# A retention layer and its feed-forward product: the output product in seven block products, and a new order on every engine

## The chip, the cores and the metric

The kernel runs on one core of a Trainium2 chip. The metric is the time of one execution on the device in microseconds (us); lower is better. Five kinds of engine work side by side, each through its own list of instructions in order: PE multiplies matrices (its weight loads are shown apart, as PEld), DVE is the vector engine, ACT the scalar engine, POOL the GpSimd engine, and SP issues the DMA transfers. An instruction starts when it is at the head of its engine's list and the results and buffers that it needs are ready.

## The reference

The inputs are q, k and v of shape (4, 8, 768, 64): batch, heads, tokens, head size. Each head keeps a state that decays by its own factor at each token, and the output of that goes through four weight matrices.

```
gamma = 1.0 - 2.0 ** (-5.0 - np.arange(H, dtype=np.float32))
scale = 1.0 / np.sqrt(D)
for t in range(S):
    state = gamma[None, :, None, None] * state + np.einsum('bhd,bhe->bhde', k[:, :, t], v[:, :, t])
    y[:, :, t] = scale * np.einsum('bhd,bhde->bhe', q[:, :, t], state)
...
x = np.ascontiguousarray(attn_out.transpose(0, 2, 1, 3)).reshape(B * S, H * D)   # 3072 x 512
a = x @ w1        # 512 x 1024
b = x @ w2        # 512 x 1024
h = a * b @ w3    # (a * b) @ w3, 1024 x 1024
return h @ w_out  # 1024 x 512
```

`w3` and `w_out` have nothing between them, so the kernel multiplies them once (`W3O`, 1024 x 512); the result is `(a * b) @ W3O`.

## The kernel before

The 3072 tokens are worked through in twelve **steps** of 256, numbered 0 to 11; three steps make one batch element, and the state is carried from step to step within it. All matrix operands are in 16-bit floats (f16), all sums in 32-bit floats in PSUM, the memory that PE writes. PSUM has eight banks, named in the code by tags (F0, F1, F2, K, S0, S1, X0, X1).

A step has these parts, each a function that is named in the program's text with the step's number first:

- `load` fetches q, k and v into tiles of a pool (`stage`, NSTAGE of them); `cast` makes f16 of q and k, `cast_v` does that for v and multiplies by a decay table (VN); `dma_turn` transposes q and k with a DMA. Without a wait list, what orders these is SP's own list.
- `kv` and `state` carry the state on, `scores` and `mask` make the masked products within a step, `inter` and `av` add up the attention output in PSUM, and `x_out` brings it to SBUF as `XT`, multiplied there on DVE by the decay of the query's token (YN).
- The two products `a` and `b` for steps 2 to 11 are done by a scheme of the Strassen and Winograd kind. A plain product of 2 x 2 blocks takes eight block products; this scheme takes seven. `combine` makes four differences of weight blocks once (`WT`), `sums` makes four sums or differences of `XT` in every step, `prod(n, u, i)` is block product i of half u, and `seed`, `keep_part`, `c12` and `c22` put the seven together in PSUM and SBUF. `half_h` multiplies a and b to give a quarter of `HT`. In the program, `rows` does the same for steps 0 and 1 with plain products.
- The output product of step n is `o_unit(n, 0)` and `o_unit(n, 1)` (line 627): eight matmuls each, of 128 weights columns by 512 output columns (in steps 4 and 7, sixteen by 256 columns). `o_copy` (line 658) brings the result to SBUF, scaled, and `o_store` or `o_store_all` writes it out.

The order on each engine is the order of the calls in the text. Up to the first part of step 3 the calls are written out one after the other; from there a loop `for n in range(3, 12)` runs the same order in each step: attention of step n, output product of step n - 1, then the fourteen `prod` of step n (in `quick`). Helper functions `tt` (line 65) and `copy` (line 62) issue most of the work of DVE, POOL and ACT, so that in the profile many groups share these two lines and are told apart by their tiles: `sodd` and `seven` are the results of `sums`, `c` of `c12` (on DVE, one input in PSUM) and `c22` (on POOL, both inputs in SBUF), `ht` of `half_h`, `u` and `p` of `keep_part`, `t` and `s` of `state`, `wt` of `combine`, `am` of `mask`, `v` of `cast_v`, `q` and `k` of `cast`.

In a step of the loop POOL has seven or eight instructions: `c22` twice, the fourth of `sums`, the last `state` (in two steps of three), and the casts of q, k and v. DVE has the other three `sums`.

## Time and profile before

| what | before |
| --- | --- |
| median of 3 runs | 176.74 us (176.43 to 178.31) |
| profiled execution, span from the first to the last instruction | 175.2 us |
| PE busy | 167.0 us (95%) |
| DVE busy | 123.8 us (71%) |
| POOL busy | 95.0 us (54%) |
| ACT busy | 88.4 us (50%) |
| read from device memory, written to it | 29.36 MB, 6.29 MB |

The profile is of one execution; its own time is the span of 175.2 us, and the median of the runs is 1.5 us longer, part of which lies around the span. A row of the profile names the line of the code, the engine, the operation, what is written and read by the program's tile names, the shapes, the count, and then busy time and the mean duration of one. "Idle before, releaser" is the time that the engine stood idle ahead of such instructions, and what it waited for.

### The profile page before, as it was taken

The numbers are of one execution on the slowest core, as the hardware profiler recorded it, in microseconds if no ns is written. First come the engines' busy times: TensorE is split into PE (matmuls) and PEld (weight loads), VectorE is DVE, ScalarE is ACT, GpSimd is POOL, SyncE is SP. The second block draws the span as 40 slices with busy tenths as digits, with TensorE's granted clock in tenths as the row PEclk, the third lists the DMA queues.
The fourth block names the chain that finished last, engine by engine and source line by source line (L and its number), as shares of the span: only waits on it lengthen the run. The fifth ranks groups of instructions, "written<-read, shape, count | busy, mean of one in ns | idle before, by whom it ended". The sixth has DMA issues, their size and how long they took to land.

```text
span 175.2 us, 7306 instructions
## 1 busy us (share of the span) xinstructions
PE 167.0 (95%) x3196; PEld 135.9 (78%) x3196; DVE 123.8 (71%) x230; ACT 88.4 (50%) x160; POOL 95.0 (54%) x124
## 2 busy tenths in 40 slices
PE   7769999999999998999999999999999999999993
PEld 2349987878877698498799986959999598695972
DVE  0454168989899758777968689686796868956370
ACT  2025986534426884182561835618357183471832
POOL 3872267866054826079584792957819366123150
PEclk9999999999999999999999999999999999999999
DMA  5999999999999989998999999999991354092563
GB/s 206 396 418 361 314 324 344 410 391 292 282 218 218 248 187 241 146 221 182 181 241 184 163 235 165 229 183 187 195 179 24 64 201 167 9 397 80 237 247 121
DMA packets 76160, 39.80 MB, mean 227 GB/s; under 512 B 53088, under 2 KB 71776, under 8 KB 76128
## 3 DMA queue, kind: packets, MB, share of 16 engines
q1 hardware_dynamic: 76128, 39.33, 93.6%
q8 instruction: 25, 0.41, 1.0%
q14 instruction: 7, 0.06, 0.1%
HBM read 29.36 MB, written 6.29 MB: 204 GB/s over the span
## 4 chain that ended last, share of the span: by engine, by line
PE 74%; DMA 11%; SPq 9%; POOL 2%; ACT 1%; issue 1%; ACTq 0%
PE psF L752 24%; PE psF L627 9%; PE psX L627 8%; PE psK L752 5%; PE psS L627 5%; DMA st<-in_v_dram 5%; PE psX L752 5%; SPq L98 5%; SPq L85 4%; DMA st<-in_q_dram 3%; PE psF L604 3%; DMA st<-in_moe_w_dram 3%; PE psX L499 2%; PE psS L604 2%; PE psF L639 2%; PE psX L525 2%
## 5 line engine op out<-in xcount | busy, mean ns | idle before, releaser
L752 PEld LDWEIGHTS <-wt 128*128 128x128 f16 x640 | 37.4, 98 | 0.0
L627 PEld LDWEIGHTS <-ht 128*128 128x128 f16 x224 | 20.8, 98 | 14.6
L65 POOL TENSOR_TENSOR c<-u,p 128x512 f32<-128x512 f32 x20 | 25.1, 1277 | 10.9 <-DVE ht L65 9.0
L752 PEld LDWEIGHTS <-w 128*128 128x128 f16 x480 | 28.9, 98 | 2.1 <-issue 0.3
L62 ACT COPY u<-psF 128x512 f32<-128x512 f32 x40 | 23.4, 591 | 7.4 <-PE psF L752 7.3
L65 POOL TENSOR_TENSOR seven<-xt,seven 128x256 f16<-128x256 f16 x9 | 6.0, 672 | 33.5 <-PE psF L752 26.3
L65 POOL TENSOR_TENSOR v<-st,VN 128x1024 f16<-128x1024 f32 x9 | 17.2, 1907 | 4.4 <-PE psX L377 4.4
L752 PE MATMUL psF<-sodd,wt 128*128 128x128 f16 x240 | 18.1, 219 | 0.0
L65 DVE TENSOR_TENSOR c<-psK,u 128x512 f32<-128x512 f32 x10 | 6.9, 691 | 15.4 <-PE psK L752 13.7
L627 PE MATMUL psF<-w3o,ht 128*128 128x256 f16 (+1 forms) x96 | 17.2, 327 | 0.0
L546 DVE TENSOR_TENSOR xt<-psX,YN 128x512 f16<-128x512 f32 x18 | 11.6, 686 | 6.2 <-PE psX L525 6.2
L65 DVE TENSOR_TENSOR ht<-psF,c 128x512 f16<-128x512 f32 x20 | 13.7, 687 | 2.5 <-POOL c L65 2.1
L658 ACT ACTIVATE osb<-psF 128x512 f32<-128x512 f32 x8 | 4.8, 597 | 20.9 <-PE psF L627 18.3
L627 PE MATMUL psX<-w3o,ht 128*128 128x512 f16 (+1 forms) x80 | 15.2, 336 | 0.0
L65 DVE TENSOR_TENSOR ht<-psX,c 128x512 f16<-128x512 f32 x19 | 13.1, 691 | 1.9
L62 POOL CAST k<-st 128x1024 f16<-128x1024 f32 x9 | 9.4, 1046 | 8.2 <-DMA st<-in_k_dram 8.2
L604 PEld LDWEIGHTS <-w 128*128 128x128 f16 x128 | 12.1, 98 | 2.2 <-POOL w L62 0.4
L276 PEld LDWEIGHTS <-w3t 128*128 128x128 f16 x128 | 12.0, 98 | 1.4
L752 PE MATMUL psX<-xt,w 128*128 128x128 f16 x152 | 11.6, 219 | 0.0
L403 DVE TENSOR_TENSOR am<-psS,keep 128x512 f16<-128x512 f32 x17 | 10.9, 681 | 0.0
L752 PE MATMUL psF<-xt,w 128*128 128x128 f16 x160 | 10.6, 219 | 0.0
L752 PE MATMUL psF<-seven,wt 128*128 128x128 f16 x160 | 10.6, 219 | 0.0
(151 smaller groups left out, 353.7 us busy)
## 6 DMA issues: line engine op xcount, KB each, us to landing
st<-in_moe_w_dram SPq DMA_DIRECT2D x16, 512.0 KB, 7.7
st<-in_q_dram SPq DMA_DIRECT2D x12, 512.0 KB, 6.6
st<-in_k_dram SPq DMA_DIRECT2D x18, 256.0 KB, 5.2
st<-in_v_dram SPq DMA_DIRECT2D x18, 256.0 KB, 4.9
out_dram<-osb SPq DMA_DIRECT2D x9, 512.0 KB, 4.9
st<-in_moe_w_out_dram SPq DMA_DIRECT2D x4, 512.0 KB, 7.7
st<-in_k_dram SPq DMA_DIRECT2D x3, 512.0 KB, 10.9
st<-in_v_dram SPq DMA_DIRECT2D x3, 512.0 KB, 8.0
```

What stands on the lines that cost most here:

```text
L62: {"v": nc.vector.tensor_copy, "g": nc.gpsimd.tensor_copy, "s": nc.scalar.copy}[eng](dst, src)
L65: (nc.vector if eng == "v" else nc.gpsimd).tensor_tensor(dst, a, b, op)
L85: via.dma_start(t[:, :].rearrange("p (h x) -> p h x", x=2 * D), src.rearrange("h (p t) d -> p h (t d)", t=2))
L98: nc.sync.dma_start(t[:, :], src[i * 128 : (i + 1) * 128, :])
L276: nc.tensor.matmul(acc[f][:, cols], lhsT=w3t[f][:, g * 128 : (g + 1) * 128], rhs=WO[i][:, r, cols], start=(first and (r, c) == (0, 0)), st ...
L403: nc.vector.tensor_tensor(t[:, :, :, :].rearrange("p a s i -> p (a s) i"), ps[:, :, :, :].rearrange("p a s i -> p (a s) i"), keep64[:, :]. ...
L499: nc.tensor.matmul(dst, lhsT=TS[n, c][half(r), a, :], rhs=rhs, start=((g, o) not in begun), stop=False, skip_group_check=True,)
L546: nc.vector.tensor_tensor(XT[n][:, :, :, :].rearrange("p t a (s x) -> p (a s) t x", s=2)[:, :, :, g * 32 : (g + 1) * 32], x[:, :, :].rearr ...
L604: nc.tensor.matmul(rows_ps[w, n, uh][j // 2][:, j % 2, :], lhsT=W[d][:, f * 128 : (f + 1) * 128], rhs=XT[n][:, :, d, :], start=(first and ...
L627: nc.tensor.matmul(ps[:, x * w : (x + 1) * w], lhsT=HT[n][:, tb, f, :], rhs=W3O[f][:, c0 + x * w : c0 + (x + 1) * w], start=(f == 0 and x ...
L658: nc.scalar.activation(o_tile(n, tb)[:, c0:c1], o_ps.pop((n, tb, c0, c1))[:, :], AF.Copy, scale=final_scale)
L752: nc.tensor.matmul(ps[:, j, :], lhsT=lhsT, rhs=rhs, start=(opens and j == 0 and c == 0), stop=(i in (2, 3, 4) and j == 3 and c == 1), skip ...
```

## The change

The change leaves the result as it is and does three things.

**The output product.** For steps 2 to 10 it is done in seven block products (`oprod`), with the same scheme as a and b. `out_combine` makes four differences of blocks of W3O once. `h_sum` makes four sums or differences of blocks of `HT` in each step, on DVE or POOL, each of 128 x 512 f16 with both inputs in SBUF. Each `oprod` is four matmuls with 256 output columns. `oseed` copies a partial sum from bank to bank, `okeep` (three of them), `o11` and `o21` bring 128 x 256 pieces to SBUF on ACT, `o12` does so on DVE with an addition, and `o22` adds two pieces in SBUF. Step 11 keeps `o_unit`, and steps 0 and 1 keep what they had.

**The query's decay.** From step 6 on (`PRE = 6`) the query is multiplied by its decay in `cast`, by a table QS, and `x_out` is then a plain copy on ACT, not a multiplication on DVE. The cast of q in steps 7 to 11 is on POOL, that of step 6 on DVE.

**The order.** The loop is gone: all calls from the first to the last are written out in a new order, for every engine, with other banks, and with the engine of each `sums`, `keep_part`, `c22`, `h_sum` and `o22` chosen call by call. The pool `stage` has 16 tiles, not 18. `scores` opens its accumulation only with the first matmuls of a bank.

```diff
-    NSTAGE = 18
+    NSTAGE = 16
+    PRE = 6
...
+        nc.scalar.activation(QS[:, :, :], vs_x[:, :, :], AF.Exp, scale=-1.0)
...
-        if nm == "q" or n < EO:
+        if nm == "q" and n >= PRE:
+            tt(
+                eng, t[:, :, :].rearrange("p t (h d) -> p h t d", d=D),
+                src[:, :].rearrange("p (h t d) -> p h t d", t=2, d=D),
+                QS[:, :, :].rearrange("p t h -> p h t").unsqueeze(3).broadcast_to((128, H, 2, D)), MULT,
+            )
+        elif nm == "q" or n < EO:
             copy(
                 eng, t[:, :, :].rearrange("p t (h d) -> p h t d", d=D),
                 src[:, :].rearrange("p (h t d) -> p h t d", t=2, d=D),
...
-                            rhs=qchunk(n, r, a, s, g), start=True, stop=True,
+                            rhs=qchunk(n, r, a, s, g), start=(a == 0 and s == 0), stop=True, skip_group_check=True,
...
+        elif n >= PRE:
+            nc.scalar.copy(
+                XT[n][:, :, :, :].rearrange("p t a (s x) -> p (a s) t x", s=2)[:, :, :, g * 32 : (g + 1) * 32],
+                x[:, :, :].rearrange("p a (s t i) -> p (a s) t i", s=2, t=2),
+            )
         else:
             nc.vector.tensor_tensor(
...
+    OT = {}
+
+    def blocks(r, c):
+        return W3O_all[:, 4 * r : 4 * r + 4, c * 256 : c * 256 + 256]
+
+    def out_combine(i, eng="v"):
+
+        if i < 3:
+            if 0 not in OT:
+                OT[0] = const.tile([128, 2, 4, 256], HP, tag="YS", name="ot12")
+            t = OT[0][:, i - 1, :, :]
+        else:
+            t = wpool.tile([128, 4, 256], HP, name=f"ot{i}")[:, :, :]
+        OT[i] = t
+        a, b = {
+            1: lambda: (blocks(0, 1), blocks(0, 0)),
+            2: lambda: (blocks(1, 1), OT[1]),
+            3: lambda: (blocks(1, 1), blocks(0, 1)),
+            4: lambda: (blocks(1, 0), OT[2]),
+        }[i]()
+        tt(eng, t, a, b, SUB)
+
+    HS = {}
+
+    def h_of(n, t, u):
+        return HT[n][:, t, 4 * u : 4 * u + 4, :]
+
+    def h_sum(n, i, eng="v"):
+
+        if i < 3:
+            t = const.tile([128, 4, 128], HP, tag=("col_f", "pos_f")[i - 1], name="hs")
+        else:
+            t = fsb.tile([128, 4, 128], HP, tag=f"hs{i}", name="hs", bufs=1)
+        HS[n, i] = t
+        a, b, op = {
+            1: lambda: (h_of(n, 0, 0), h_of(n, 0, 1), ADD),
+            2: lambda: (HS[n, 1][:, :, :], h_of(n, 1, 0), SUB),
+            3: lambda: (h_of(n, 1, 0), h_of(n, 0, 0), SUB),
+            4: lambda: (h_of(n, 1, 1), HS[n, 2][:, :, :], SUB),
+        }[i]()
+        tt(eng, t[:, :, :], a, b, op)
+
+    OB, ov = {}, {}
+
+    def oprod(n, i, tag=None):
+
+        key = {1: "A", 6: "A", 7: "A", 4: "A", 5: "B", 3: "B", 2: "C"}[i]
+        if i in (1, 5):
+            OB[n, key] = bank(tag, [128, 256])
+        ps = OB[n, key]
+        lhs, rhs = {
+            1: lambda: (h_of(n, 1, 0), blocks(0, 0)),
+            2: lambda: (h_of(n, 1, 1), blocks(1, 0)),
+            3: lambda: (HS[n, 4], blocks(1, 1)),
+            4: lambda: (h_of(n, 0, 1), OT[4]),
+            5: lambda: (HS[n, 1], OT[1]),
+            6: lambda: (HS[n, 2], OT[2]),
+            7: lambda: (HS[n, 3], OT[3]),
+        }[i]()
+        for f in range(4):
+            nc.tensor.matmul(
+                ps[:, :], lhsT=lhs[:, f, :], rhs=rhs[:, f, :], start=(i in (1, 5) and f == 0),
+                stop=(i in (2, 3, 4) and f == 3), skip_group_check=True,
+            )
+
+    def oseed(n, tag):
+        OB[n, "C"] = bank(tag, [128, 256])
+        nc.scalar.copy(OB[n, "C"][:, :], OB[n, "A"][:, :])
+
+    def scaled(dst, src):
+        nc.scalar.activation(dst, src, AF.Copy, scale=final_scale)
+
+    def okeep(n, name):
+        if name == "p5":
+            t = fsb.tile([128, 256], FP, tag="op5", name="op5", bufs=1)[:, :]
+        else:
+            t = o_tile(n, {"u2": 1, "u3": 0}[name])[:, 256:512]
+        ov[n, name] = t
+        scaled(t, OB[n, {"u2": "A", "u3": "A", "p5": "B"}[name]][:, :])
+
+    def o_done(n, k):
+        o_n[n] = o_n.get(n, 0) + 256
+
+    def o11(n):
+        scaled(o_tile(n, 1)[:, 0:256], OB.pop((n, "C"))[:, :])
+        o_done(n, 1)
+
+    def o21(n):
+        scaled(o_tile(n, 0)[:, 0:256], OB.pop((n, "A"))[:, :])
+        o_done(n, 0)
+
+    def o12(n):
+        nc.vector.scalar_tensor_tensor(
+            o_tile(n, 1)[:, 256:512], OB.pop((n, "B"))[:, :], final_scale, ov.pop((n, "u2")), MULT, ADD
+        )
+        o_done(n, 1)
+
+    def o22(n, eng="g"):
+        tt(eng, o_tile(n, 0)[:, 256:512], ov.pop((n, "u3")), ov.pop((n, "p5")), ADD)
+        o_done(n, 0)
...
-    for n in range(3, 12):
-        inter(n, 0, ("X0", "X1"))
-        fence(n)
-        if n == 11:
-            o_unit(10, 0, ("S0",))
-            o_copy(10, 0)
-        else:
-            kv(n + 1, ("K", "F2"), (0,))
-            if n == 3:
-                dma_turn("k", 5)
-                dma_turn("q", 5)
-                fetch("v6")
-                load("k", 7)
-                load("q", 7)
-            scores(n + 1, ("S0", "S1"))
-            kv(n + 1, ("K", "F2"), (1,))
-        inter(n, 1)
-        av(n)
-        x_out(n, 0)
-        x_out(n, 1)
-        if n < 11:
-            half_h(n - 1, 1, 1)
-        sums(n, 1)
-        if n < 11:
-            for i in range(1, 5):
...
+    h_sum(7, 3)
+    inter(8, 1)
+    av(8)
+    half_h(7, 1, 1)
+    dma_turn('q', 11)
+    kv(9, ('K', 'F2'), (1,))
+    scores(9, ('S0', 'S1'))
+    x_out(8, 1)
+    o_store_all(5)
+    h_sum(7, 1)
+    oprod(7, 1, 'X0')
+    x_out(8, 0)
+    state(9, 1)
+    oprod(7, 5, 'F0')
+    dma_turn('k', 10)
+    h_sum(7, 2)
+    oseed(7, 'X1')
+    sums(8, 3, 'g')
+    prod(8, 0, 1, 'F1')
+    state(9, 2)
+    oprod(7, 6)
+    state(9, 3)
+    sums(8, 1, 'g')
+    oprod(7, 2)
+    mask(9, 1)
+    okeep(7, 'u2')
+    sums(8, 2, 'g')
+    prod(8, 0, 5, 'K')
+    state(9, 4)
+    seed(8, 0, 'S1')
+    oprod(7, 7)
+    cast('q', 10, 'g')
+    mask(9, 0)
+    okeep(7, 'p5')
+    prod(8, 1, 5, 'F2')
+    o11(7)
+    sums(8, 4)
+    prod(8, 0, 6)
+    keep_part(8, 0, 'p5', 'v')
+    okeep(7, 'u3')
+    keep_part(8, 1, 'p5')
+    prod(8, 1, 1, 'S0')
+    h_sum(7, 4)
+    prod(8, 0, 3)
+    cast_v(11, 'g')
...
```

What that does to the lists of instructions is shown at three places of step 8. On PE, the output product of step 7 stands in the list of before as whole rows of one kind, each with 256 or 512 columns (`w3o` are the blocks of W3O, `ht` the blocks of HT; the rows shown open the first of the two units):

```order
L627 LDWEIGHTS ht
L627 MATMUL psF_3413<-w3o_107,ht 128x256
L627 LDWEIGHTS ht
L627 MATMUL psF_3413<-w3o_107,ht 128x256
L627 LDWEIGHTS ht
```

In the list of the change the seven products are spread among the products of a and b. Here is the end of the first (`oprod(7, 1)`), and the start of the fifth, whose weights `hs` come from `h_sum(7, 1)` and whose other operand `ot` comes from `out_combine`:

```order
L736 LDWEIGHTS ht
L736 MATMUL psX_3528<-w3o,ht 128x256
L736 LDWEIGHTS hs
L736 MATMUL psF_3536<-ot_1372,hs 128x256
L736 LDWEIGHTS hs
L736 MATMUL psF_3536<-ot_1372,hs 128x256
```

So four of the seven products (3, 5, 6 and 7) have weights that DVE or POOL make in the same step; the 32 matmuls of this step's output product are now 28.

On DVE, step 8 in the list of before, from the two `x_out` (`xt<-psX,YN`) to the masks and the first of `c12`:

```order
L546 TENSOR_TENSOR xt<-psX_3251,YN 128x8x2x32
L546 TENSOR_TENSOR xt<-psX_3252,YN 128x8x2x32
L65 TENSOR_TENSOR ht<-psF_3116,c_3223 128x512
L65 TENSOR_TENSOR sodd<-xt 128x256
L62 CAST t_3394<-psK 128x256
L65 TENSOR_TENSOR t_3396<-psF_3272,t_3394 128x256
L65 TENSOR_TENSOR t_3398<-psK,t_3396 128x256
L65 TENSOR_TENSOR s_3400<-psF_3272,t_3398 128x256
L65 TENSOR_TENSOR sodd<-xt 128x256
L65 TENSOR_TENSOR seven<-xt,sodd 128x256
L403 TENSOR_TENSOR am<-psS_3289,keep_85 128x512
L403 TENSOR_TENSOR am<-psS_3290,keep_85 128x512
```

And the same stretch in the list of the change, where `hs` are the four `h_sum` of step 7, and `seven` the one of `sums` that DVE still has in this step:

```order
L66 TENSOR_TENSOR hs<-ht 128x512
L66 TENSOR_TENSOR ht<-psF_3222,c_3365 128x512
L66 TENSOR_TENSOR hs<-ht 128x512
L63 CAST t_3534<-psK 128x256
L66 TENSOR_TENSOR hs<-hs,ht 128x512
L66 TENSOR_TENSOR t_3559<-psF_3370,t_3534 128x256
L66 TENSOR_TENSOR t_3565<-psK,t_3559 128x256
L413 TENSOR_TENSOR am<-psS_3490,keep_85 128x512
L66 TENSOR_TENSOR s_3586<-psF_3370,t_3565 128x256
L413 TENSOR_TENSOR am<-psS_3489,keep_85 128x512
L66 TENSOR_TENSOR seven<-xt,seven 128x256
L63 COPY p_3619<-psK 128x512
```

The two `x_out` have left DVE, two of the three `sums` have gone to POOL, and three `h_sum` (of four) and a `keep_part` have come.

POOL's list of before for step 8: the cast of k, the fourth of `sums`, the last `state`, the casts of v and q, and two `c22`:

```order
L62 CAST k_3402<-st 128x1024
L65 TENSOR_TENSOR seven<-xt,seven 128x256
L65 TENSOR_TENSOR t_3407<-s_3400,GS 128x256
L65 TENSOR_TENSOR v_3452<-st,VN 128x1024
L62 CAST q_3454<-st 128x8x2x64
L65 TENSOR_TENSOR c_3552<-u_3550,p_3498 128x512
L65 TENSOR_TENSOR c_3574<-u_3572,p_3526 128x512
```

POOL's list of the change for the same step, from the cast of v10 to that of k11:

```order
L66 TENSOR_TENSOR v_3418<-st,VN 128x1024
L66 TENSOR_TENSOR sodd<-xt 128x256 x2
L66 TENSOR_TENSOR seven<-xt,sodd 128x256
L66 TENSOR_TENSOR q_3594<-st,QS 128x8x2x64
L66 TENSOR_TENSOR v_3643<-st,VN 128x1024
L66 TENSOR_TENSOR c_3701<-u_3690,p_3619 128x512
L63 CAST k_3744<-st 128x1024
```

Three `sums` stand there now, the cast of q has become a product of two tensors, and two casts of v fall into this step.

1276 lines of the change are left out of this document (933 added, 343 removed).

## The prediction

> **What bounds the kernel now.** I read the page's first part, then the busy time by stretches cut at the start of each step's attention (step 3 begins at 68.72 us), then the chain that ended last. Columns behind the stretch: its length, then busy time (and count) of PE, PEld, DVE, ACT and POOL, the granted clock, and DMA's share and rate.
>
> ```profile
> PE 167.0 (95%) x3196; PEld 135.9 (78%) x3196; DVE 123.8 (71%) x230; ACT 88.4 (50%) x160; POOL 95.0 (54%) x124
> ...
> 68.72:80.68 11.96, 11.16 (x250) 9.02 (x249) 8.78 (x18) 6.62 (x12) 6.83 (x7) 1.00 1.19 186
> ...
> 91.78:102.85 11.07, 11.07 (x274) 10.57 (x272) 8.65 (x17) 5.57 (x11) 7.30 (x7) 1.00 1.06 182
> 102.85:113.80 10.95, 10.95 (x250) 8.96 (x248) 8.74 (x17) 5.57 (x11) 7.57 (x8) 1.00 1.43 207
> ...
> 135.90:146.94 11.04, 11.04 (x252) 9.01 (x251) 8.82 (x18) 5.57 (x11) 6.04 (x7) 1.00 0.49 167
> ...
> 62.95 6.12 DMA st<-in_q_dram
> 69.10 1.04 ACT q L62
> 70.37 0.28 PE psX L499 x9
> ...
> 82.03 1.83 PE psF L627 x8
> 83.86 1.73 PE psX L627 x8
> 85.59 0.89 PE psF L752 x16
> ...
> 93.07 1.85 PE psF L627 x16
> 94.92 1.75 PE psX L627 x16
> ```
>
> From step 4 on PE is busy in the whole of every step, 11.0 us each, and its pieces in the chain follow without a hole: PE is the bound. DVE needs 8.7 to 8.8 us of a step, POOL 6.0 to 7.6, ACT 5.6. Step 3 has one hole of about 1.1 us, where a fence on ACT stands behind a cast that waits for q.
>
> **What the change takes from PE.** An output product now costs 1.83 + 1.73 = 3.56 us, and 3.60 us with sixteen times two matmuls of 256 columns. The last is 0.1125 us per matmul of 256 columns; 28 of them are 3.15 us. So PE loses 0.41 us in seven steps and 0.45 us in two, **3.8 us in all**, if nothing makes it wait. The matmuls stay as they were in kind, so I see no reason for another price.
>
> **What it gives to DVE.** Spacing first.
>
> ```profile
> 106.19 0.42 DVE L65 TENSOR_TENSOR t<-psK,t 128x256 f16<-128x256 f32 x1
> 106.64 0.42 DVE L65 TENSOR_TENSOR t<-psF,t 128x256 f16<-128x256 f32 x1
> ...
> 108.43 1.28 DVE L403 TENSOR_TENSOR am<-psS,keep 128x512 f16<-128x512 f32 x2
> ...
> L403 DVE TENSOR_TENSOR am<-psS,keep 128x512 f16<-128x512 f32 x17 | 10.9, 681 | 0.0
> L65 DVE TENSOR_TENSOR wt<-w,wt 128x1024 f16<-128x1024 f16 x4 | 2.7, 686 | 0.0
> ```
>
> Two masks take 1.28 us and one 0.68, so instructions of 512 columns follow each other every 0.60 us; `state` every 0.45. I counted the list of the change for steps 3 to 9, seven steps. There are 74 of 512 columns (28 `half_h`, 14 `c12`, 14 masks, 8 `keep_part`, 6 `x_out`, 4 `c22`): 44.4 us. 26 `state`: 11.7. 10 `o12` and `o22` of 256 columns at 0.42: 4.2. 12 `sums` at 0.28 (median, below): 3.4. 19 `h_sum` of 512 f16 columns, which no row shows: between 0.28 (256 columns) and 0.69 (1024), I take 0.41 on the straight line: 7.8. Two casts that multiply 1024 columns: 0.69 to twice 0.60, I take 1.2: 2.4. **Sum 73.9 us**, against 60.6 before (the seven stretches, 8.78 to 8.82). PE's own sum for these steps is 78.2 - 1.1 - 2.9 = 74.2 us. So DVE comes level with PE before anything goes wrong.
>
> **What it gives to POOL.** In the same seven steps:
>
> ```profile
> L65 POOL TENSOR_TENSOR c<-u,p 128x512 f32<-128x512 f32 x20 | 25.1, 1277 | 10.9 <-DVE ht L65 9.0 <-ACT u L62 1.9
> L65 POOL TENSOR_TENSOR v<-st,VN 128x1024 f16<-128x1024 f32 x9 | 17.2, 1907 | 4.4 <-PE psX L377 4.4
> L62 POOL CAST q<-st 128x1024 f16<-128x1024 f32 x8 | 8.3, 1042 | 3.1 <-DMA st<-in_q_dram 3.1
> L65 POOL TENSOR_TENSOR seven<-xt,seven 128x256 f16<-128x256 f16 x9 | 6.0, 672 | 33.5 <-PE psF L752 26.3 <-DVE seven L65 7.2
> L65 POOL TENSOR_TENSOR t<-s,GS 128x256 f16<-128x256 f32 x8 | 5.8, 731 | 0.1
> ```
>
> 16 `sums` at 0.67, 11 `c22` at 1.28, 10 `h_sum` at 1.28 (same width, f16 and not f32; twice 0.67 is the other bound, 1.34), 11 products of 1024 columns (6 of v, 5 of q) at 1.91, 9 of 256 f32 columns at 0.73, 3 plain casts at 1.04: 68 us, against 51 before. POOL runs nine tenths of the time in which it stood idle a third, above all ahead of the `sums` (33.5 us in nine).
>
> **What these two do to each other** decides the case. Rows of `wt` and `sodd` by tile (duration in ns: least, median, longest), then the neighbours in time of the longest:
>
> ```profile
> L65 DVE TENSOR_TENSOR wt<-w,w x4: 677/688/1525, 40.8 to 47.9; 128x1024 f16<-128x1024 f16 x4
> L65 DVE TENSOR_TENSOR sodd<-xt x20: 279/281/442, 60.5 to 162.1; 128x256 f16<-128x256 f16 x20
> ...
> 40.80 2.73 DVE L65 TENSOR_TENSOR wt<-w,w 128x1024 f16<-128x1024 f16 x3
> 41.00 1.39 POOL L62 CAST w<-st 64x1024 f16<-64x1024 f32 x1 [0.24 <-DMA st<-in_moe_w_dram]
> ...
> 83.16 1.06 POOL L62 CAST k<-st 128x1024 f16<-128x1024 f32 x1
> 83.92 0.44 DVE L65 TENSOR_TENSOR sodd<-xt 128x256 f16<-128x256 f16 x1
> ...
> 47.92 0.68 DVE L65 TENSOR_TENSOR wt<-w,w 128x1024 f16<-128x1024 f16 x1
> 48.03 2.36 POOL L65 TENSOR_TENSOR v<-st,VS 128x1024 f16<-128x1024 f32 x1 [5.64 <-DMA st<-in_v_dram]
> ...
> 99.90 0.69 DVE L65 TENSOR_TENSOR c<-psK,u 128x512 f32<-128x512 f32 x1 [1.24 <-PE psK L752]
> 100.70 0.69 DVE L65 TENSOR_TENSOR ht<-psX,c 128x512 f16<-128x512 f32 x1
> 98.96 1.91 POOL L65 TENSOR_TENSOR v<-st,VN 128x1024 f16<-128x1024 f32 x1
> ```
>
> The cast of k ends at 84.22, and a `sodd` that began under it ends at 84.36, 0.44 us long and not 0.28: it was held to the end of the cast. The second `wt` at 41.4 lasts 1.53 us, to 42.93, 0.54 behind the end of the cast of w. The other way round, the product of v at 48.03 lasts 2.36 us, 0.45 more than its like at 98.96, under a `wt` that runs to 48.60. But `c` and `ht`, with one input in PSUM, take their 0.69 us under POOL's work. So DVE instructions with **both inputs in SBUF** and POOL instructions exclude each other, whole instruction by whole instruction. Before, this cost next to nothing, since POOL waits while DVE makes `sums`.
>
> The change has 40 such instructions on DVE in the seven steps (19 `h_sum`, 12 `sums`, 4 `c22`, 3 `o22`, 2 casts), beside a POOL that is nearly always in one. An arrival at random finds an instruction of duration d running with chance d/T and waits d/2 for it; with the durations above the sum of d squared is 90, so a wait is 45/T. With T = 90 us that is 0.50 us. In about a quarter of the 40, POOL itself stands waiting for their result (`sums` 3 for `sums` 2, `h_sum` 1 for `h_sum` 2), so 30 waits: 15 us. **DVE then needs 73.9 + 15 = 89 us where the seven steps took 78.2: 10.5 us more.** Nothing hides it: PE's four products on `hs`, its eight on `sums` and the banks that `c12` and `half_h` free all stand behind DVE's list. Step 8 by hand says the same: `h_sum(7, 1)` is held by the cast of v and `sums(8, 3)`, which costs PE some 1.5 us ahead of `oprod(7, 5)`; `sums(8, 4)` is held by the products of q and v (3.8 us together), which costs 1.2 us ahead of `prod(8, 0, 3)`. The bounds: no wait at all (74), all 40 waits (94).
>
> [...] Read narrowly, the rows show DVE held by casts alone; of these POOL keeps only three in the seven steps, and the sum would be 74. [...]
>
> **The rest.**
>
> ```profile
> DMA  5999999999999989998999999999991354092563
> ...
> L658 ACT ACTIVATE osb<-psX 128x512 f32<-128x512 f32 x8 | 4.8, 597 | 9.1 <-PE psX L627 9.1
> ```
>
> In steps 10 and 11 the change gives POOL nothing to do, so there PE keeps its gain: 2 x 0.41 = 0.8 us off. Up to step 3 the same weights arrive in another order; the differences of blocks, now twelve and shared by DVE and POOL, may collide too, and the first useful work may come sooner: -1.5 to +1.5, I take 0. On ACT a step gets six copies of 256 columns and, from step 6 on, two `x_out`, and loses two `o_copy`; even at the 0.60 us of the 512 columns of `osb` that is 3.6 us more, and ACT has 5.4 idle us in a step. Sixteen tiles in the pool make SP's list wait longer for a free one, and the transposes behind it with it; DMA's busy share (tenths in 40 slices) falls off at slice 31, 131 us, three steps ahead of PE's end, so I cost it at nothing, with 1 us per late load if that is wrong.
>
> **Sum**: 175.2 + 10.5 - 0.8 = 184.9 us of span; the median of the runs lies 1.5 us above the span: **186 us**.
>
> **Rivals.** (a) The holds fall into gaps of POOL: the seven steps take 74 to 77 us, PE's and DVE's sum and some friction, and the time is 176.7 - 0.8 - (1.2 to 4.2) = 171.7 to 174.7 us. For it: POOL waits for DVE often, and the sums of both allow it. Against it: of the 40, 35 stand in the written order behind a POOL instruction that would still be running. (b) Shorter holds, about 0.18 us each: 40 x 0.18 = 7 us, 81 us, and 178.7 in the end. The point from which the change loses is a mean hold of 0.13 us. (c) POOL starts its next instruction ahead of a DVE that is held: two `c22` in a row are 1.23 us apart, less than one's 1.28. Then a hold may span two POOL instructions, waits double, and it is beyond 195 us. (d) The products don't come cheaper: excluded by the rows of 256 columns.
>
> **Chances.** Forecast, 181 to 191 us: 0.50. (b), 175 to 181: 0.20. (a), below 175: 0.23. (c) and worse, above 191: 0.07. One per cent of 176.74 is about what this kernel's runs can tell from no change: faster than 175.0 has 0.23, within it 0.10 (half of (b)), slower 0.67. The range 172 to 191 leaves out some 0.1 below and 0.07 above.
>
> **What would show it.** PE's busy share falls below 90% and the steps of 3 to 9 are near 12.7 us long; `hs` on DVE has a mean well above 0.41 us and a longest near 2; POOL's `sums` show durations above 0.67; steps 10 and 11 have no such rows. If `hs` takes 0.4 us throughout and PE stays busy, the prediction is wrong, and (a) holds.

## The result, and the profile after

The changed kernel takes **206.03 us** (median of 4 runs, 205.76 to 207.16) against 176.75 us before: **1.164 times as long**, with a 95% interval of 1.158 to 1.170. The forecast was 186 us. Some executions of a kernel run a few per cent longer at a lower granted clock (of the kernel before, one took 183.97 us at a mean of 0.972 and one 176.48 at 1.000); the medians and ratios here leave them out. The direction is as forecast, the size is not: the profiled span is 203.9 us, 19.0 us longer than the 184.9 of the sum.

First the page's first part, and the stretches from the attention of step 3 to the end, cut where the attention of a step starts (length, then busy time and count of PE, PEld, DVE, ACT and POOL, granted clock, DMA's share and rate):

```profile
PE 174.8 (86%) x3272; PEld 145.5 (71%) x3272; DVE 170.5 (84%) x274; ACT 103.9 (51%) x206; POOL 113.8 (56%) x129
...
77.17:93.78 16.61, 12.52 (x333) 11.13 (x337) 16.54 (x22) 9.23 (x18) 11.54 (x10) 1.00 0.54 117
93.78:110.50 16.72, 12.75 (x284) 11.66 (x280) 15.08 (x23) 6.87 (x15) 9.51 (x9) 0.90 0.83 170
110.50:124.37 13.87, 11.02 (x245) 9.81 (x241) 13.49 (x21) 6.04 (x14) 11.49 (x10) 1.00 0.65 138
...
162.73:176.76 14.03, 12.56 (x342) 10.87 (x329) 12.95 (x22) 7.43 (x17) 8.85 (x10) 1.00 0.32 104
176.76:203.90 27.14, 23.92 (x424) 21.24 (x411) 19.32 (x43) 16.09 (x35) 0.00 (x0) 1.00 0.20 75
```

PE no longer fills a step; DVE does, almost. The steps of 11.0 us have become 12.4 to 16.7. Measured from the start of the attention of step 3 to that of step 10 (the seven steps below), and ahead of and behind that:

| us | up to the attention of step 3 | seven steps | rest | span |
| --- | --- | --- | --- | --- |
| before | 70.5 | 77.2 | 27.5 | 175.2 |
| after | 77.2 | 99.6 | 27.1 | 203.9 |
| difference | +6.7 | +22.4 | -0.3 | +28.8 |
| forecast | 0 | +10.5 | -0.8 | +9.7 |

The rows by tile (duration in ns: least, median, longest), and then three holds in the timeline with the POOL row above which each stands:

```profile
L66 DVE TENSOR_TENSOR hs<-ht x15: 410/930/2283, 76.7 to 190.4; 128x512 f16<-128x512 f16 x15
L66 DVE TENSOR_TENSOR hs<-ht,hs x6: 413/687/1800, 87.9 to 191.1; 128x512 f16<-128x512 f16 x6
L66 DVE TENSOR_TENSOR sodd<-xt x11: 276/289/1932, 68.0 to 189.3; 128x256 f16<-128x256 f16 x11
...
82.81 2.28 DVE L66 TENSOR_TENSOR hs<-ht 128x512 f16<-128x512 f16 x1
82.69 2.12 POOL L66 TENSOR_TENSOR ot<-w3o,ot 128x1024 f16<-128x1024 f16 x1
...
107.89 1.53 DVE L66 TENSOR_TENSOR hs<-ht 128x512 f16<-128x512 f16 x1
107.86 1.27 POOL L66 TENSOR_TENSOR c<-u,p 128x512 f32<-128x512 f32 x1 [0.98 <-POOL osb L66]
...
99.99 2.12 DVE L66 TENSOR_TENSOR osb<-osb,op 128x256 f32<-128x256 f32 x1
99.74 2.08 POOL L66 TENSOR_TENSOR v<-st,VN 128x1024 f16<-128x1024 f32 x1
```

An unheld `h_sum` takes 0.41 us, as guessed; the longest takes 2.28. In the seven steps 28 DVE rows last more than 0.1 us longer than the shortest of the same operation and shape, by 23.6 us together, **0.84 us each**. (The texts that were written ahead of the experiments say 22.8 us.) The first POOL instruction that such a row meets ends 0.14 to 0.55 us before the row does (1.08 us for a cast of q with two inputs, at 85.35, which takes 1.22 us by itself); none is held over two. In the three rows shown POOL began only 0.03 to 0.25 us earlier than the DVE instruction that it holds. Over all 28, a held instruction comes a third of the way into the POOL instruction, on average, and none comes later than 0.68 of it.

### The profile page after: what moved, and what is told of

It is laid out like the page before. It is cut to its first block, busy times and chain, and to the rows that moved or that the text cites. A ratio compares the mean times of both kernels' runs of the same rounds, so it can differ in the third digit from the quotient of the medians.

```text
span 203.9 us, 7573 instructions
## 1 busy us (share of the span) xinstructions
PE 174.8 (86%) x3272; PEld 145.5 (71%) x3272; DVE 170.5 (84%) x274; ACT 103.9 (51%) x206; POOL 113.8 (56%) x129
## 4 chain that ended last, share of the span: by engine, by line
PE 40%; DVE 35%; issue 8%; DMA 8%; POOL 4%; SPq 3%; ACT 1%; DVEq 0%; ACTq 0%
DMA st<-in_moe_w_dram 8%; PE psF L867 7%; DVE ht L66 5%; PE psX L867 5%; DVE hs L66 5%; PE psS L867 4%; PE psF L736 3%; DVE t L66 3%; PE psK L867 3%; DVE am L413 3%; PE psX L736 3%; DVE sodd L66 2%; PE psS L641 2%; DVE wt L66 2%; SPq L86 2%
## 5 line engine op out<-in xcount | busy, mean ns | idle before, releaser
L66 POOL TENSOR_TENSOR c<-u,p 128x512 f32<-128x512 f32 x12 | 16.0, 1341 | 9.8 <-ACT u L63 5.8
L736 PEld LDWEIGHTS <-hs 128*128 128x128 f16 x144 | 12.9, 98 | 6.5 <-DVE hs L66 3.9
L66 DVE TENSOR_TENSOR hs<-ht 128x512 f16<-128x512 f16 x15 | 14.9, 990 | 0.1
L66 POOL TENSOR_TENSOR v<-st,VS 128x1024 f16<-128x1024 f32 x3 | 6.2, 2082 | 13.1 <-ACT QS L207 11.9
L280 PEld LDWEIGHTS <-w3t 128*128 128x128 f16 x128 | 11.9, 98 | 1.7 <-DVE w3t L63 0.2
L63 ACT COPY u<-psF 128x512 f32<-128x512 f32 x14 | 8.1, 588 | 9.1 <-PE psF L867 9.1
L619 PE MATMUL psF<-xt,w 128*128 128x256 f16 x48 | 9.5, 284 | 3.0 <-DVE ht L66 3.0
L736 PEld LDWEIGHTS <-ht 128*128 128x128 f16 x108 | 9.4, 98 | 3.2 <-DVE ht L66 1.6
L736 PE MATMUL psF<-ot,hs 128*128 128x256 f16 x56 | 8.3, 273 | 2.7 <-DVE hs L66 2.4
L746 ACT ACTIVATE osb<-psF 128x256 f32<-128x256 f32 x19 | 7.3, 386 | 6.0 <-PE psF L736 6.0
L66 POOL TENSOR_TENSOR q<-st,QS 128x1024 f16<-128x1024 f32 x5 | 9.7, 1941 | 0.0
L280 PE MATMUL psF<-wo,w3t 128*128 128x256 f16 x64 | 9.0, 273 | 0.0
```

Of the source, the lines that this page charges most:

```text
L63: {"v": nc.vector.tensor_copy, "g": nc.gpsimd.tensor_copy, "s": nc.scalar.copy}[eng](dst, src)
L66: (nc.vector if eng == "v" else nc.gpsimd).tensor_tensor(dst, a, b, op)
L280: nc.tensor.matmul(acc[f][:, cols], lhsT=w3t[f][:, g * 128 : (g + 1) * 128], rhs=WO[i][:, r, cols], start=(first and (r, c) == (0, 0)), st ...
L619: nc.tensor.matmul(rows_ps[w, n, uh][j // 2][:, j % 2, :], lhsT=W[d][:, f * 128 : (f + 1) * 128], rhs=XT[n][:, :, d, :], start=(first and ...
L736: nc.tensor.matmul(ps[:, :], lhsT=lhs[:, f, :], rhs=rhs[:, f, :], start=(i in (1, 5) and f == 0), stop=(i in (2, 3, 4) and f == 3), skip_g ...
L746: nc.scalar.activation(dst, src, AF.Copy, scale=final_scale)
```

## The experiments

### What holds what, measured alone

A kernel with nothing of the layer in it runs ten or so equal DVE instructions beside equal POOL instructions on tiles of their own. On DVE, `two` is a sum of 512 f16 columns with both inputs in SBUF, `cast` makes f16 of 512 f32 columns with one input in SBUF, and `psum` adds 512 f32 columns with one input in PSUM. On POOL, `add` adds 512 f32 columns, `gcast` casts 1024, and `set` is a memset of 512.

```diff
+        "two": lambda: nc.vector.tensor_tensor(sh[:, :], ha[:, :], hb[:, :], ADD),
+        "cast": lambda: nc.vector.tensor_copy(sc[:, :], fb[:, :]),
+        "psum": lambda: nc.vector.tensor_tensor(sf[:, :], ps[:, :], fb[:, :], ADD),
...
+        "add": lambda: nc.gpsimd.tensor_tensor(gc[:, :], pa[:, :], pb[:, :], ADD),
+        "gcast": lambda: nc.gpsimd.tensor_copy(gk[:, :], fa[:, :]),
+        "set": lambda: nc.gpsimd.memset(gm[:, :], 0.5),
```

> This kernel leaves the whole computation out: it only runs rows of one kind of DVE instruction beside rows of one kind of POOL instruction, each kind also alone, on tiles that nobody else uses. Theory L (a lock held for a whole instruction, taken in turn): sums of 512 f16 columns with both inputs in SBUF take 0.41 us alone, and beside a POOL that adds 512 f32 columns without a pause (1.28 us each) they come one for one with POOL's, 1.7 us apart, each showing about 1.7 us; a sum with an input in PSUM stays at 0.69 us. What the prediction held, that only two inputs in SBUF count, makes a cast with one input in SBUF run at its own time beside POOL; the casts of the weights in the trace of the change (1.11 us and not 0.77) speak for a hold there too. Beside a POOL that only writes (memset) there is nothing to read, and the sums should stay at 0.41 us. Theory R (arrivals at random, as the prediction priced a hold): the mean wait beside a POOL that is always busy is half an instruction, 0.64 us, so sums show about 1.05 us.

The timeline's rows, first a sum (`sh`) and an add alone, then sums beside adds, a sum between instructions on PSUM, casts beside adds, instructions on PSUM beside adds, sums beside casts of POOL, and sums and casts beside memsets:

```profile
7.25 4.56 DVE L89 TENSOR_TENSOR sh<-ha,hb 128x512 f16<-128x512 f16 x10 [5.31 <-ACT sh L103]
23.99 7.96 POOL L94 TENSOR_TENSOR gc<-pa,pb 128x512 f32<-128x512 f32 x6 [21.38 <-ACT gc L103]
...
44.55 10.27 DVE L89 TENSOR_TENSOR sh<-ha,hb 128x512 f16<-128x512 f16 x8 [21.70 <-ACT sh L103]
44.87 13.75 POOL L94 TENSOR_TENSOR gc<-pa,pb 128x512 f32<-128x512 f32 x10 [0.80 <-ACT gc L103]
...
66.63 1.40 DVE L91 TENSOR_TENSOR sf<-ps,fb 128x512 f32<-128x512 f32 x2
67.95 1.50 DVE L89 TENSOR_TENSOR sh<-ha,hb 128x512 f16<-128x512 f16 x1
...
79.50 10.24 DVE L90 CAST sc<-fb 128x512 f16<-128x512 f32 x8 [4.56 <-ACT sc L103]
94.38 7.21 DVE L91 TENSOR_TENSOR sf<-ps,fb 128x512 f32<-128x512 f32 x10 [4.64 <-ACT sf L103]
105.91 8.77 DVE L89 TENSOR_TENSOR sh<-ha,hb 128x512 f16<-128x512 f16 x8 [4.31 <-ACT sh L103]
118.35 6.40 DVE L89 TENSOR_TENSOR sh<-ha,hb 128x512 f16<-128x512 f16 x14 [3.68 <-ACT sh L103]
125.85 8.39 DVE L90 CAST sc<-fb 128x512 f16<-128x512 f32 x12 [1.10 <-ACT sc L103]
```

Sums alone stand 0.46 us apart. Beside adds seven of them (the first finds POOL idle) stand 1.40 us apart: (10.27 - 0.46) / 7. POOL's adds, 1.26 us each, go from 1.34 us apart, (7.96 - 1.26) / 5, to 1.39, (13.75 - 1.26) / 9. So they take turns (the lock of theory L, as it is called below), and **DVE pays 0.94 us a turn, POOL 0.05**. The expected 1.7 us was too much: by the single rows the next add starts 0.2 us before the held sum ends. Why the two may overlap there is not shown. Theory R falls with the mixed rows: a sum after two instructions on PSUM does not meet POOL anywhere in its add, but at its start every time but the first, and takes 1.50 us and not 0.42. That it is the start lies in the lengths: the two instructions on PSUM take 1.33 us (63.88 to 65.21), one add with its gap 1.34, so that each hold leads to the next. In the change, where other work lies between, a held instruction meets POOL elsewhere: a third of the way in, on average (above). A cast with one input is held like a sum (seven stand 1.40 us apart, too; alone they stand 0.46 apart); the prediction's "both inputs in SBUF" was too narrow. Instructions on PSUM stay 0.72 us apart, unheld. Casts on POOL hold sums too (1.2 us apart). Beside memsets sums are free (0.46 apart), casts are not: 12 in 8.39 us, of which ten meet a memset and stand 0.74 apart. What makes memsets slow the casts (0.74 us apart, and 0.46 alone) and not the sums (0.46 both ways), no row shows.

### The change without the lock

POOL's instructions compute two columns, to wait for the same inputs, and then write the whole result with memsets, which have no input and beside which the sums above stood 0.46 us apart, as they do alone. That leaves nearly all of POOL's computation out, keeps the order, and nearly keeps POOL's busy time.

```diff
     def tt(eng, dst, a, b, op):
+        if eng == "g" and blank:
+            nc.gpsimd.tensor_tensor(few(dst), few(a), few(b), op)
+            nc.gpsimd.memset(dst, 0.01)
+            nc.gpsimd.memset(dst, 0.01)
+            return
```

The second run leaves the last memset out, the third does it on a part of the result only.

> The change, in which from the first casts of w1 on every POOL instruction is made of one that computes two columns (so that it waits for the same inputs) and of memsets of the whole result, two for a sum or product and one for a cast, which keep POOL about as long busy (0.3 us for 256 columns in the trace) but read nothing; nearly all of what POOL computes is left out. Theory L: DVE's instructions with both inputs in SBUF lose their excess (22.8 us in steps 3 to 9). DVE then needs 71.8 us there and PE 74, so the seven steps take 75 to 80 us, the part up to step 3 some 3 to 5 us less than the 77.2 of the change, and the whole 176 to 182 us. Theory O (the new order itself, its chains of waits from engine to engine, with POOL's work as long as before): it stays at 195 us or more. In between, 182 to 195, the two share it.

> The change without the lock, as in the run before with memsets in POOL's place, but with one memset for each sum or product and not two: POOL's instructions are about half as long as in the change, wait for the same inputs, and still leave nearly all of POOL's computation out. With the lock gone, steps 3 to 9 took 85.8 us, 8.6 more than before the change. Theory P (what is left comes from POOL's own slowness, which delays sums and h_sum for PE): the seven steps fall to 81 us or less, the whole to some 179 us. Theory C (what is left is the coupling of two lists, DVE with 72 us and PE with 74 us of work, in a fixed order): they stay at 84 to 86 us, the whole at 184 us or more.

> The first run without the lock again, with the second memset of each sum or product cut so that a POOL instruction lasts as long as the one it replaces (c22 1.27 us, the product of v 1.91, a sum of 256 columns 0.6 to 0.7, a cast 1.2); in the first run most were 0.1 to 0.3 us longer. Nearly all of POOL's computation is left out again. With POOL's instructions a little too long steps 3 to 9 took 85.8 us, with them at half 82.2. If POOL's length counts beside the lock, they take 83 to 85 us here and the whole is 182 to 186 us; what is left between that and the 99.6 of the change is the lock's.

The stretch of the seven steps of the change, and then of the first, second and third run, and the `hs` rows of the third:

```profile
77.17:176.76 99.59, 82.65 (x1918) 73.74 (x1921) 94.58 (x144) 50.19 (x110) 71.70 (x61) 0.98 0.68 154
```

```profile
72.89:158.66 85.77, 79.17 (x1919) 72.56 (x1921) 71.27 (x143) 49.85 (x110) 74.37 (x179) 1.00 0.93 189
```

```profile
69.87:152.05 82.18, 77.76 (x1918) 72.53 (x1921) 70.74 (x144) 49.71 (x110) 46.01 (x122) 1.00 0.99 200
```

```profile
71.10:152.51 81.41, 77.93 (x1919) 72.70 (x1921) 70.77 (x143) 49.74 (x110) 60.59 (x155) 1.00 0.99 199
...
L86 DVE TENSOR_TENSOR hs<-ht x15: 414/416/425, 70.7 to 166.2; 128x512 f16<-128x512 f16 x15
```

The holds are gone (`hs` takes 0.42 us, and no DVE row of the seven steps is more than 0.1 us longer than the shortest of its kind), and DVE's busy time falls from 94.6 to 70.8 us. In the third run POOL is as long in its list as in the change: 60.6 us busy and some 94 more gaps of 0.06 us (the run of pairs has memsets of 0.52 us that stand 0.58 apart) are 66, and 71.7 less 5.0 in which it was held itself are 67. The span is 179.7 us and the median 181.6 us (1.029 times before, 1.021 to 1.036). So of the 28.8 us **the lock makes 24.2**: 18.2 in the seven steps, 6.1 in the start. That holds what follows from its waits, such as the stretches at half clock below; by the first run it would be 18.0 (13.8 and 4.3). The first run's expectation (75 to 80 us for the steps) was too low all the same: without any hold they take 81.4, 4.2 more than before. With POOL half as long nothing more is won (82.2; median 180.5), while with POOL some 0.1 to 0.3 us too long in most instructions they take 85.8 (median 187.2): POOL's list is at the edge of setting the pace.

### The old start

The kernel before up to the end of step 3 (with the four `out_combine` on DVE in steps 2 and 3), and the order of the change from the attention of step 4 on. The lines are against the kernel before.

```diff
     mask(3, 0)
+    out_combine(1)
+    out_combine(3)
...
+    mask(4, 1)
+    out_combine(2)
+    out_combine(4)
...
+    inter(4, 0, ('F1', 'F0'))
```

> The kernel before up to the end of step 3 (its order, its output product of steps 0 to 2 as rows), the four differences of output weights put into steps 2 and 3 on DVE, and from the attention of step 4 on the order of the change. If the loss up to step 3 (6.7 us from the first instruction to the attention of step 3, 5.6 more in the step behind it) belongs to the new order of the start, and the loss of steps 4 to 9 to the order there, then the attention of step 4 comes at about 83 us and not 93.8, the steps behind it are as long as in the change (16.7, 13.9, 13.1, 12.9, 12.4, 14.0), and the time is about 195 us. If the early delay only pushed work together that then collides (a late start that makes later holds), steps 4 to 9 get shorter too, towards 11 to 12 us each, and the time is 185 or less.

195.8 us (1.096 times before, 1.085 to 1.108), as the first theory had it. The attention of step 4 starts at 84.1 us and not 93.8, and the steps behind it last 16.7, 13.9, 13.1, 12.8, 12.4 and 14.0 us, each within 0.02 us of the change's own. The steps carry nothing over from the start; the two losses are separate.

### The old order with the sums alone

The kernel before with the four `h_sum` of steps 3 to 9 put on DVE, used by nobody; then the same with POOL's work replaced by memsets, 1.1 us a step too long at first, then of the right length.

```diff
         if n < 11:
             half_h(n - 1, 1, 1)
+        if 3 < n < 11:
+            h_sum(n - 1, 4)
...
         quick(n, ("F1", "F0"), ("K", "F2"), ("X0", "X1"))
+        if n < 10:
+            h_sum(n, 1)
+            h_sum(n, 2)
+            h_sum(n, 3)
```

> The kernel before, its order and its output product in rows, with nothing but the four h_sum of steps 3 to 9 put on DVE (nobody uses them): three at the end of a step behind half_h, where DVE has idle time, the fourth behind the last half_h of the step, in the next one. They add 1.64 us to the 8.7 that DVE needs in a step of 11.0. Theory H (hidden): a step stays at 11.0 to 11.2 us, the time at 176 to 178 us. Theory L (the lock makes each wait for a POOL instruction that runs there, c22 or the cast of k): DVE gets 2 to 4 us of holds in a step, h_sum shows means near 1 us, a step takes 11.6 to 12.8 us, and the time is 180 to 188 us.

> The kernel before with the four h_sum added on DVE, as in the earlier run, and from step 3 on POOL's instructions made of two computed columns and memsets of the same length (most of what POOL computes is left out). With POOL's real work a step was 12.4 to 13.7 us from step 4 on, where it is 11.0 without h_sum. Theory L (the lock makes most of that): the holds go, DVE has 10.3 us of work in a step, and the steps are 11.0 to 11.6 us. If the place of the h_sum in DVE's list makes it (1.64 us of work ahead of the copies that PE waits for), the steps stay at 12.2 us or more.

> The old order with the four h_sum on DVE and POOL's work from step 3 on replaced by memsets of the same length, cut in the same way (most of what POOL computes is left out). With POOL's real work the stretch from the attention of step 3 to that of step 10 took 88.8 us, with memsets that were 1.1 us a step too long 88.2, both against 77.2 without h_sum. Theory K (a step is one round of waits: the fourth of sums, the casts and c22 on POOL, then half_h, h_sum, x_out and sums on DVE, so that POOL's length and DVE's holds both count): the stretch falls by the holds in it, 8.3 us less what was not on that round, to 80 to 84 us. If the place of h_sum alone makes the loss, it stays at 87 to 89 us.

In these three profiles the unchanged part ahead of step 3 ran 3 to 7 us longer than in that of before, so only the seven steps are compared. In that part the granted clock stood at half for 10.2 us in the first, 3.4 us in the second and 6.8 us in the third, which explains at most half of these times, 5.1, 1.7 and 3.4 us of the delay (at 0.50 four matmuls of 512 columns take 1.91 us in the change, at 1.00 the same take 1.03 in the run with plain queries); the rest is open. In the seven steps it is 1.00 in all three. They are, in this order:

```profile
77.18:166.00 88.82, 78.72 (x1792) 66.46 (x1792) 76.52 (x142) 38.97 (x77) 51.75 (x47) 1.00 0.83 153
```

```profile
73.51:161.66 88.15, 79.05 (x1791) 66.49 (x1792) 68.82 (x140) 38.97 (x77) 54.74 (x123) 1.00 0.92 155
```

```profile
75.72:157.12 81.40, 78.35 (x1790) 66.39 (x1792) 69.53 (x142) 38.96 (x77) 48.44 (x113) 1.00 1.00 167
```

The sums alone cost the old order 11.6 us, with no change in its output product (190.7 us; 1.077 times before, 1.048 to 1.107). DVE is held 13 times in them, all `hs`, by 7.4 us together, under `c22` and under the casts of k and q; without the holds and with POOL's length kept, the steps take 81.4, so the holds cost 7.4 us and the sums without them 4.2. The middle run shows that POOL's length counts as well: with no hold, but POOL 1.1 us longer in a step, the loss was back. Rows of one step of the first of the three, by time, show a round:

```profile
134.79 0.29 DVE L65 TENSOR_TENSOR seven<-xt,sodd 128x256 f16<-128x256 f16 x1
135.25 0.67 POOL L65 TENSOR_TENSOR seven<-xt,seven 128x256 f16<-128x256 f16 x1 [5.14 <-DVE seven L65]
135.88 1.90 POOL L65 TENSOR_TENSOR v<-st,VN 128x1024 f16<-128x1024 f32 x1
...
138.77 2.51 POOL L65 TENSOR_TENSOR c<-u,p 128x512 f32<-128x512 f32 x2
...
140.08 0.69 DVE L65 TENSOR_TENSOR ht<-psF,c 128x512 f16<-128x512 f32 x1
140.69 0.88 DVE L65 TENSOR_TENSOR hs<-ht 128x512 f16<-128x512 f16 x1
141.60 1.14 DVE L65 TENSOR_TENSOR hs<-hs,ht 128x512 f16<-128x512 f16 x1
```

The fourth of `sums` on POOL waits 5.14 us for DVE's; the product of v, the cast of q and `c22` stand behind it on POOL; `half_h` needs the first `c22` (to 140.05), and `h_sum`, then `x_out` and the next `sums`, stand behind that on DVE. Holds on DVE lengthened the steps (88.8 us), and so did a longer POOL (88.2), as theory K says; its forecast, 80 to 84 us without either, was met.

### What the steps of the change wait for

First, products 3, 5, 6 and 7 of the output take HT itself, so that nobody waits for an `h_sum` (another output); second, the same with memsets in POOL's place (first form); third, nine `keep_part` moved from DVE to ACT.

```diff
-            5: lambda: (HS[n, 1], OT[1]),
+            5: lambda: (h_of(n, 0, 0), OT[1]),
...
-    keep_part(4, 1, 'u2', 'v')
+    keep_part(4, 1, 'u2')
```

> The change, in which products 3, 5, 6 and 7 of the output take blocks of HT itself and not the h_sum (so the output is another one); the h_sum are still made, on the same engines at the same places, and nobody waits for them. Theory D (the steps last as long as DVE's list, with its holds: 94.6 of 99.6 us busy): steps 3 to 9 take 96 to 99 us, the whole 200 to 203. Theory W (PE's waits for hs make the loss): PE's 8 long waits at these products go, the steps take 92 us or less, the whole 196 us or less.

> Both at once: POOL's work replaced by memsets of the same length (most of POOL's computation left out), and products 3, 5, 6 and 7 of the output taking HT itself. Without the lock DVE has some 14 us of idle time in the seven steps and PE waits 11.4 us. If these waits are for hs (theory W), the seven steps fall from 85.8 to 80 us or less. If they are spread over all that DVE makes, the masks, HT and the banks it frees (theory C), they stay at 84 us or more.

> The change, in which the nine keep_part that stand on DVE from step 4 on (0.69 us each, eight of them between the attention of step 4 and that of step 10) are on ACT, which is idle 40% of the time. Nothing else moves. Theory D (the steps last as long as DVE's list with its holds): the stretch of 99.6 us loses what DVE loses, 4 to 5.5 us, and the time is 200 to 202 us. Rival (the steps last as long as chains of waits through ACT, PE and POOL in which DVE is one link): 2 us or less, or a loss, since ACT's list gets longer: 204 us or more.

The seven steps of the three runs:

```profile
78.06:177.51 99.45, 81.91 (x1918) 73.77 (x1921) 94.19 (x144) 50.17 (x110) 71.70 (x61) 0.98 0.71 154
```

```profile
73.16:157.57 84.41, 78.63 (x1919) 72.83 (x1921) 71.19 (x143) 49.74 (x110) 74.35 (x179) 1.00 0.90 185
```

```profile
77.21:175.00 97.79, 82.91 (x1919) 73.40 (x1921) 91.33 (x136) 53.79 (x118) 71.42 (x61) 0.98 0.71 157
```

Taking PE's waits for `hs` away changes next to nothing (99.45 for 99.59 in the profile, whose span, 204.8 us, is the longest of this run's four; median 204.0 us, 1.154 times before, 1.138 to 1.170): theory W, which had 196 us or less, falls. Without the lock it wins 1.4 us (85.8 to 84.4; median 186.3), so that what is left there is not those waits either. But theory D, by which a step is as long as DVE's list, falls as well: eight instructions of 0.69 us less on DVE, 5.5 us, shorten the steps by 1.8 us only (median 204.2 us, 1.147 times before). DVE's busy time fell by 3.3 and not by 5.5, part of it since the holds grew, from 23.6 us in 28 rows to 24.9 in 29.

### Plain queries

```diff
-    PRE = 6
+    PRE = 12
```

> The change without its second part: the query keeps its decay at the output of the attention on DVE in every step, and its cast is plain. Theory L with DVE as the bound: DVE gets two instructions of 0.6 us more in each step from 6 on, POOL's cast of q falls from 1.93 to 1.04 us in five of them and so holds DVE less, by some 0.3 to 0.5 us a step: steps 6 to 9 are longer by 0.5 to 1 us each, the two last steps too, and the time is 207 to 211 us. If POOL's load is what matters most (a POOL with 0.9 us less in a step comes out of DVE's way), the time is 200 to 204 us.

205.4 us (1.150 times before, 1.141 to 1.159), between the two expectations: counted from attention to attention, steps 3, 4 and 5 are shorter by 0.5, 2.2 and 0.9 us, steps 8 and 9 longer by 1.7 and 0.7, the rest behind them by 2.0, and the start is 2.2 us shorter, 1.7 of it in one stretch for a reason of its own, the clock, told at the end. The clock bears on step 4 as well: in the change it is at half there for 3.4 us, in this run nowhere in the steps. The second part of the change explains none of the loss.

## Why the prediction was right and wrong

- **The mechanism: right.** Holds of DVE under POOL, forecast from a few rows of before, make 24.2 of the 28.8 us. That POOL's sums and products hold DVE as its casts do, on which the forecast's sum rests, no row of the prediction shows. The runs do: beside adds sums stand 1.40 us apart and not 0.46, and in the change `hs` takes 1.53 us under a `c22` and `osb` 2.12 under a product of v (above). Of what was to show it, `hs` has a mean near 1 us and a longest of 2.28, PE's share is 86%, POOL's `sums` take up to 0.85 us, and the last two steps have no such rows; the steps are 14.2 us long on average and not 12.7.
- **The price of the holds: the first wrong step.** The forecast had 30 waits at 0.50 us, 15 us; there were 28 holds at 0.84, 23.6 us. The step that failed is "An arrival at random finds an instruction of duration d running with chance d/T and waits d/2 for it", together with the quarter that was then taken off the 40. POOL has 68 us of work in a T of 90, so that chance d/T already leaves out the time in which POOL runs nothing; the quarter, for a POOL that waits, counted that a second time. Without it the same sum is 40 x 0.50 = 20 us. In the trace 39 such instructions start in the seven steps. 28 of them, 72%, began while POOL was in an instruction, which is POOL's busy share, and all 28 were held; the other 11 began while it was in none. What is left is that they came early: the POOL instructions that they met last 1.44 us on average, and 0.97 us of that was left, where from the middle it is 0.72. Why they come early no run takes apart; one of them comes straight out of a hold into the next POOL instruction (99.99).
- **The base: the second wrong step.** "DVE then needs 73.9 + 15" took DVE's list for the length of the steps. The list itself was nearly right: 94.6 - 23.6 = 71.0 us, and 70.8 in the run without holds. But that run's seven steps take 81.4 us, not 74: DVE stands idle for 10.6 us of them and PE for 3.5. 81.4 and the lock's 18.2 make the 99.6, where the forecast had 73.9 and 15. The steps of rival (a), 74 to 77 us, were not reached even without holds.
- **The start: the third wrong step.** The twelve differences of blocks that "may collide too" were costed at 0 within 1.5 us; the start lost 6.7, and the lock makes 6.1 of it. Rows of the start, DVE first, then POOL, then PE:

```profile
46.15 2.02 DVE L66 TENSOR_TENSOR wt<-w,w 128x1024 f16<-128x1024 f16 x1
49.28 4.21 DVE L66 TENSOR_TENSOR wt<-w,wt 128x1024 f16<-128x1024 f16 x2
...
45.42 2.19 POOL L66 TENSOR_TENSOR wt<-w,w 128x1024 f16<-128x1024 f16 x1
48.30 2.12 POOL L66 TENSOR_TENSOR wt<-w,wt 128x1024 f16<-128x1024 f16 x1 [0.69 <-ACT VN L221]
50.38 2.56 POOL L66 TENSOR_TENSOR wt<-w,w 128x1024 f16<-128x1024 f16 x1
...
54.15 0.58 PE L619 MATMUL psF<-xt,w 128*128 128x256 f16 x2 [2.98 <-DVE ht L66]
```

  Three `combine` that take 0.69 us alone took 6.2 us, and `ht` stood behind them, for which PE waited 2.98 us; the clock then fell to half, as told at the end. The same arithmetic as for `h_sum` was at hand and not applied.
- **The price of a product on PE: right.** A product takes 0.44 us (four matmuls, to the next in line), forecast 0.45; it is not visible, since PE waits:

```profile
178.50 0.60 PE L736 MATMUL psS<-w3o,ht 128*128 128x256 f16 x4
178.93 0.60 PE L736 MATMUL psX<-ot,hs 128*128 128x256 f16 x4
```

- **The rest.** In steps 10 and 11, without POOL, 0.3 us were won and not 0.8. Rival (c), holds over two POOL instructions, did not come up: none of the 28 is one. The differences from the forecast are +6.7 (start), +11.9 (steps: 7.5 of base, 3.2 of the lock, 1.0 since the forecast's seven steps, cut a little elsewhere, were 78.2 us before and not 77.2, and 0.2 since 73.9 + 15 - 78.2 is 10.7 and not 10.5) and +0.5 (end), which is the 19.0 us but for 0.1 of rounding.
- **Still open:** why the order without any hold needs 81.4 us where the forecast gave PE 74 us of work; PE shows 77.9 us busy there. No run took that apart, and the trace of the lock-free run puts part of PE's idle time to nothing that it shows. No version here beats the kernel before; even without the lock the change takes 1.029 times as long.

## What to carry to other kernels

Work that is moved from PE to DVE and POOL is paid where those two meet: count the DVE instructions that read SBUF only, casts too, and price each that meets a busy POOL at well over half of a POOL instruction (here 0.84 of 1.44 us, and 0.94 of 1.26 in the run of pairs). POOL's busy share was the chance of meeting one here (72%, 28 of 39); do not take its idle time off twice. Then do not take the fullest engine's list for the time of a step: follow one round of waits through all engines, and add the holds to it. Work taken off the fullest engine may win little: here eight instructions of 0.69 us won 1.8 us. Apply the price everywhere that the same kind of instruction appears, the start of the program included.

## What the runs showed that was not expected

**The same wait, with and without a slower clock.** In the start of the change PE stands idle for 2.98 us, and in the run with plain queries as well, behind the same instruction. Here are four matmuls of 512 columns in the change, with stretches before and behind the end of the wait, and the same in the other run:

```profile
55.38 1.91 PE L653 MATMUL psF<-w3o,ht 128*128 128x512 f16 x4
...
50.73:54.14 3.41, 0.43 (x4) 0.23 (x3) 3.38 (x4) 0.00 (x0) 3.41 (x2) 1.00 1.14 229
54.18:57.50 3.32, 3.32 (x12) 1.69 (x12) 1.70 (x3) 0.00 (x0) 3.32 (x3) 0.50 1.20 268
```

```profile
54.45 1.03 PE L653 MATMUL psF<-w3o,ht 128*128 128x512 f16 x4
...
49.37:52.78 3.41, 1.44 (x14) 1.14 (x12) 3.38 (x2) 0.00 (x0) 3.41 (x3) 1.00 1.03 260
52.78:56.20 3.42, 2.40 (x19) 1.76 (x19) 2.75 (x5) 0.00 (x0) 3.42 (x2) 1.00 0.92 232
```

In the change the clock is 0.50 for 3.4 us, and the stretch from the attention of step 1 to that of step 2 takes 29.3 us; in the other run it stays at 1.00, and the stretch takes 27.6. A second such drop follows a wait of 2.75 us behind the attention of step 4 (the stretch with the clock of 0.90, above). So a wait of that length cost another 1.7 us in one run and nothing in the other. The traces show a pattern in it, not its cause. In the change these two drops last 3.413 us each, and the drops begin at 54.14, 101.92 and, behind the last work, 204.32 us: 14 and 30 times 3.413 us apart. Laid on a grid of that step, the wait of 2.98 us lies in one stretch, 50.73 to 54.14, in which PE is busy for 0.43 us, and the stretch ahead of the second drop, 98.51 to 101.92, has PE busy for 1.10. In the other run the one drop, behind its last work, begins at 202.97; counted back from there in steps of 3.413 us (that the step is the same there is the author's estimate from the drops of the change), the same wait is split between two stretches, in which PE is busy for 1.44 and 2.40 us, and neither is followed by a drop. So PE need not be idle for all of such a stretch. How little work is enough stays open: in the run with nine `keep_part` on ACT a drop follows such a stretch with PE busy for 1.5 us, more than the 1.44 that had none.

**Who pays.** In the run of pairs a sum on DVE and an add on POOL that take turns do not share the loss: the sums went from 0.46 to 1.40 us apart, the adds from 1.34 to 1.39. And a cast on DVE is slowed even by a memset on POOL (0.46 to 0.74 us apart), which a sum is not; there POOL pays as well, its memsets going from 0.58 to 0.74 us apart.
